# Casting the values in the DMA instead of on ScalarE, in an attention and expert kernel

## The chip, the cores and the metric

One Trainium2 chip; the kernel runs on one of its cores. The metric is the device time of one execution in microseconds. The engines are called as in the profile: PE (TensorE), ACT (ScalarE), DVE (VectorE), POOL (GpSimd) and SP (SyncE, which here only issues DMAs). SP, ACT and POOL can each issue DMAs; a DMA that changes the type of its data is issued from POOL in this kernel.

## The reference

Two layers follow each other. The first is attention with a relative-position bias; the second sends every token to one of eight experts by a hash of its id. Cut to what matters:

```python
# attention: B = 8 batches, H = 8 heads, S = 576 tokens, D = 64
scores = (1.0 / np.sqrt(D)) * np.matmul(q, k.transpose(0, 1, 3, 2))
scores = scores + bias_table[bucket(|i - j|)]        # one column of the table per head
attn = softmax(scores)
x = np.matmul(attn, v)                               # -> (B * S, H * D) = (4608, 512)

# experts: E = 8, w1 (E, 512, 1024), w2 (E, 1024, 512)
expert_idx = token_ids * 2654435761 % E
for e in range(E):
    mask = expert_idx == e
    out[mask] = np.maximum(x[mask] @ w1[e], 0.0) @ w2[e]
```

## The kernel before

The attention goes in 32 pairs of heads (8 batches x 4 pairs). The loop over `n` has one pass per pair and one more. In pass `n` the kernel computes the scores of pair `n` and the product of pair `n - 1` with its values; the inputs of later pairs are loaded, cast and transposed beside it. Keys are on the partitions, so the exponential on ACT writes the transposed attention that the value product takes as its stationary operand.

The values of a pair lie in a buffer `vt` (one of four): for each head four blocks of 128 keys, each block 64 value columns, a column of ones (its product is the softmax denominator) and zeros. The last 64 keys of a head are kept apart, in `vs`, for both heads of a pair together. Before the change v is loaded as float32 into `vf` by SP and cast into `vt` by ACT:

```python
VN = 98                       # width of a block of vt, and of the value product
vf = [at.tile([P, 2, NDUO, D], F32, name=f"vf{i}") for i in range(4)]
vt = [at.tile([P, 2 * (NDUO * VN + VO)], F16, name=f"vt{i}") for i in range(4)]

def load_v(n):
    b, m = pairs[n]
    for hh in range(2):
        nc.sync.dma_start(out=vf[n % 4][:, hh, :, :],
                          in_=v[b, 2 * m + hh, :NB4].rearrange("(t p) d -> p t d", p=P))

def cast_v(n):
    nc.scalar.activation(out=vt[n % 4][...][:, :, :, :D], in_=vf[n % 4][:, :, :, :],
                         func=AF.Copy, bias=0.0, scale=1.0)

def cast_vs(b):               # the tail of a batch, cast by POOL, two halves
    for hh in range(2):
        nc.gpsimd.tensor_copy(out=vs[b % 2][D * hh : D * hh + D, :, c0 : c0 + D],
                              in_=vsf[b % 2][D * hh : D * hh + D, :, :])
```

The scores of a group `g` go to PSUM (two buffers) and are exponentiated by ACT. `band` multiplies the part near the diagonal by the exponential of the bias, on DVE; `ebd` holds it, and `ebs` a compact copy for the last 64 keys:

```python
def scores(n, g):
    ...
    nc.scalar.activation(out=att[:, g, :, :], in_=ps[:, :, :QW], func=AF.Exp, ...)   # 128 x 1152

def band(n, g):
    ...                                       # g < 4: att *= ebd, one or two products
    nc.vector.tensor_tensor(out=a, in0=a, in1=ebs[:, :, m, :], op=ALU.mult)          # g == 4
```

At the end of a value product (`av_steps`) DVE takes reciprocals and scales. From pair 7 on POOL also clears a piece of the buffers for gathered rows there, and from pair 13 on it names slots: it scatters token numbers into a table in DRAM, one indirect DMA for each 128 tokens, 40 in all. A one-element copy of `rcp` paces them:

```python
if n >= 7 and (blank or unnamed):
    nc.gpsimd.tensor_copy(out=pace[:, :], in_=rcp[:1, 0, 0:1])
    if n >= 13:
        for _ in range(1 if ni == 2 else 2):
            if unnamed:
                name_slot(unnamed.pop(0))      # nc.gpsimd.indirect_dma_start(...)
    if blank:
        nc.gpsimd.memset(xf[...], 0)
```

The loop, cut to what the change touches:

```python
weights = [(w, e, w * y) for e in range(2) for w in (1, 2) for y in range(4)]   # 16 pieces
for n in range(NP + 1):                        # NP = 32
    av = iter(())
    if n > 0:
        av = av_steps(n - 1, finish if n == NP else None)
    if n == NP:
        first_inputs(0)                        # needs the rows gathered for expert 0
        advance(av, 99)
        ...
        break
    if 0 < n < NP - 4:
        load(n + 4, "qk" if n < 3 else "qkv")
    if b + 1 < B and m == 1: load_vs(b + 1)
    if b + 1 < B and m == 3: cast_vs(b + 1)
    if n == 28: ...                            # load the table of slots into xid
    if n >= 6 and pairs[n][1] != 0 and weights:
        w, e, y = weights.pop(0)
        (load_w1 if w == 1 else load_w2)(e, y, y + w)
    for g in range(NIT):                       # 5 groups
        scores(n, g)
        if n == NP - 2 and g == 1:
            gather(0, B - 1)                   # rows of expert 0 without the last batch
        if n == 0:
            if g == 1:   cast_k(1)
            elif g == 2: band(n, 0); band(n, 1)
            elif g == 3: transpose_q(1); transpose_k(1); band(n, 2)
            elif g == 4: band(n, 3); load(4, "qk")
        ...
        elif g == 0:
            transpose_k(n + 1); band(n - 1, NIT - 1); advance(av, 13)
        elif g == 1:
            cast_k(n + 2); cast_v(n + 1); advance(av, 14); band(n, 0)
        elif g == 2:
            cast_q(n + 3); advance(av, 9); band(n, 1)
        elif g == 3:
            transpose_q(n + 2); band(n, 2); advance(av, 99)
        else:
            band(n, 3)
```

After the loop the experts follow, one after the other: `hps` is the first product, `ops` the second, and the rows of the next expert are gathered and transposed beside them. The weights of experts 0 and 1 are loaded during attention, those of the others during the experts.

Of the kernel before, what the change touches and what calls it, by code (L numbers as in the profile page):

```python
# [31 lines left out]
def kernel(  # L32
# [145 lines left out]
    VO = HP - (VW - VN)  # L178
    NCH = S // D
# [3 lines left out]
    with tc.tile_pool(name="at", bufs=1) as at, tc.tile_pool(  # L183
# [3 lines left out]
        def aux(shape, dtype, name):  # L187
# [9 lines left out]
        qh, kh = {}, {}  # L197
        qf = [at.tile([PB, 2, NBLK, 2 * D], F32, name=f"qf{i}")
# [3 lines left out]
        vf = [at.tile([P, 2, NDUO, D], F32, name=f"vf{i}") for i in range(4)]  # L202
        vsf = [at.tile([P, NPAIR, D], F32, name=f"vsf{i}") for i in range(2)]
        vt = [at.tile([P, 2 * (NDUO * VN + VO)], F16, name=f"vt{i}")
              for i in range(4)]
# [7 lines left out]
        def load(n, what="qkv"):  # L213
            b, m = pairs[n]
            if what == "v":
                return load_v(n)
# [17 lines left out]
            if what == "qkv":  # L234
                load_v(n)

        def load_v(n):
            b, m = pairs[n]
            for hh in range(2):
                nc.sync.dma_start(  # L240
                    out=vf[n % 4][:, hh, :, :],
                    in_=v[b, 2 * m + hh, :NB4].rearrange(
                        "(t p) d -> p t d", p=P
                    ),
                )
# [25 lines left out]
        def cast_k(n):  # L271
# [4 lines left out]
            )  # L276

        def cast_v(n):
            nc.scalar.activation(  # L279
                out=vt[n % 4][:, :].rearrange("p (h y) -> p h y", h=2)[  # L280
                    :, :, : NDUO * VN
                ].rearrange("p h (t x) -> p h t x", t=NDUO)[:, :, :, :D],
                in_=vf[n % 4][:, :, :, :], func=AF.Copy, bias=0.0, scale=1.0,
            )
# [224 lines left out]
        def band(n, g):  # L509
# [22 lines left out]
            else:  # L532
# [3 lines left out]
                nc.vector.tensor_tensor(  # L536
                    out=a, in0=a, in1=ebs[:, :, m, :], op=ALU.mult
                )

        def av_steps(n, done=None):  # L540
            b, m = pairs[n]
            att, ats = atts[n]
            vb = vt[n % 4]
            for its in ((3, 4), (0, 1, 2)):
# [4 lines left out]
                for y, (ii, it, x) in enumerate(todo):  # L549
# [3 lines left out]
                    else:  # L553
# [7 lines left out]
                        v0 = (NDUO * VN + VO) * hh - VO * hh + VN * t  # L561
# [102 lines left out]
        keep_busy(bps[:, 2, :], 4)  # L664
# [8 lines left out]
        def v_init(i):  # L673
            nc.gpsimd.memset(vt[i][:, :].bitcast(I32), 0)
            nc.gpsimd.memset(
                vt[i][:, :].rearrange("p (h y) -> p h y", h=2)[
                    :, :, : NDUO * VN
                ].rearrange("p h (t x) -> p h t x", t=NDUO)[
                    :, :, :, D : D + 1
                ], 1.0,  # L680
# [18 lines left out]
        keep_busy(bps[:, 2, :], 4)  # L699
# [33 lines left out]
        for i in range(1, 4):  # L733
            v_init(i)
        nobody = at.tile([P, NSLOT // P, 2], I32, name="nobody")
        nc.gpsimd.memset(nobody[:, :, :], BIG)
        load_bias(nc.scalar, 0, 1, 0)
        load_bias(nc.sync, 0, 1, 1)
        load(0, "v")
        load_vs(0)  # L740
        load(2, "qk")
        for b2 in range(2):
            load_bias(nc.gpsimd, 1, NPAIR, b2)
        make_ebs(0, 1)
        cast_vs(0)
        make_ebs(1, NPAIR)
        transpose_q(0)
        keep_busy(bps[:, 2, :], 1)
        transpose_k(0)
        keep_busy(bps[:, 2, :], 1)  # L750
        cast_q(1)
        load(1, "v")
        load(3, "qk")
        load(2, "v")
        load(3, "v")
# [20 lines left out]
                   for e in range(2) for w in (1, 2) for y in range(4)]  # L776
        routing = route()
# [5 lines left out]
        for n in range(NP + 1):  # L783
# [9 lines left out]
            if 0 < n < NP - 4:  # L793
                load(n + 4, "qk" if n < 3 else "qkv")
            b, m = pairs[n]
            if n == 1:
                vs_init(1)
            if b + 1 < B and m == 1:
# [5 lines left out]
            if n == 28:  # L804
                assert not unnamed and not blank and not weights
# [4 lines left out]
            if n >= 6 and pairs[n][1] != 0 and weights:  # L810
                w, e, y = weights.pop(0)
                (load_w1 if w == 1 else load_w2)(e, y, y + w)
            for g in range(NIT):
# [9 lines left out]
                if n == 0:  # L823
                    if g == 1:
                        cast_k(1)
                    elif g == 2:
                        band(n, 0)
                        band(n, 1)
                    elif g == 3:
                        transpose_q(1)  # L830
                        transpose_k(1)
# [4 lines left out]
                elif n == 1:  # L836
                    if g == 0:
                        cast_v(0)
                        load_v(4)
# [13 lines left out]
                    else:  # L853
                        cast_v(1)
                        load_v(5)
# [8 lines left out]
                elif g == 1:  # L864
                    if n == 2:
                        transpose_q(3)
                        cast_v(2)
                        load_v(6)
# [239 lines left out]
```

## Time and profile before

| | us |
|---|---|
| median of three executions | 379.4 |
| the three | 378.36, 379.40, 380.87 |
| span of the profiled execution | 387.9 |
| in it: attention, to the first expert product | 231.4 |
| in it: experts | 156.5 |

The profiled execution is longer than the timed ones, so its stretches are compared with each other and with the profile of another kernel, and times with times. In a profile, a line such as `L492 ACT ACTIVATE att<-ps` is a group of instructions of line 492 on ACT that writes `att` from `ps`; a bracket at the end of a line is the idle time of that engine just before, and what ended it. The slots are named by the groups `t_id<-pay,ds`, the rows of an expert are gathered by `xg<-t_x,xid`, the attention's result is stored by `t_x<-x_all`.

| the values and what lies near them | engine | count | mean or median |
|---|---|---|---|
| exponential `att<-ps`, 128 x 1152 | ACT | 128 | 1129 ns |
| cast `vt<-vf`, 128 x 512 | ACT | 32 | 0.62 us |
| load `vf<-in_v_dram`, 128 KB | SP issues | 64 | - |
| slot `t_id<-pay,ds` | POOL | 40 | 1006 ns |
| weight piece `w1t`, 128 rows | POOL | 8 | 0.53 us |

### The profile page before, as it was taken

The numbers are of one execution on the slowest core, as the hardware profiler recorded it, in microseconds if no ns is written. First come the engines' busy times: TensorE is split into PE (matmuls) and PEld (weight loads), VectorE is DVE, ScalarE is ACT, GpSimd is POOL, SyncE is SP. The second block draws the span as 40 slices with busy tenths as digits, with TensorE's granted clock in tenths as the row PEclk, the third lists the DMA queues.
The fourth block names the chain that finished last, engine by engine and source line by source line (L and its number), as shares of the span: only waits on it lengthen the run. The fifth ranks groups of instructions, "written<-read, shape, count | busy, mean of one in ns | idle before, by whom it ended". The sixth has DMA issues, their size and how long they took to land.

```text
span 387.9 us, 8991 instructions
## 1 busy us (share of the span) xinstructions
PE 334.0 (86%) x3483; PEld 236.4 (61%) x3483; DVE 221.2 (57%) x617; ACT 241.1 (62%) x297; POOL 187.3 (48%) x300
## 2 busy tenths in 40 slices
PE   7578888898886889786887889989999999999991
PEld 2356767677675667574775676555656566665650
DVE  5679999999987999885797630303030202121121
ACT  2758888899986898784887716343535344544420
POOL 4622010131358758758625007587868585752322
PEclk9999999999999999996999899999999999999997
DMA  5999997888978998997642012939999999997212
GB/s 139 253 227 230 216 200 194 188 199 215 202 176 180 160 234 160 195 226 162 123 57 65 2 64 64 215 93 188 237 228 260 208 232 212 196 220 136 95 56 81
DMA packets 124854, 65.81 MB, mean 170 GB/s; under 512 B 85681, under 2 KB 117070, under 8 KB 124802
## 3 DMA queue, kind: packets, MB, share of 16 engines
q0 software_dynamic: 19584, 31.75, 40.4%
q1 hardware_dynamic: 104834, 33.18, 36.2%
q8 instruction: 29, 0.48, 0.5%
q10 hardware_dynamic: 384, 0.21, 0.2%
q14 instruction: 23, 0.19, 0.2%
HBM read 68.26 MB, written 15.30 MB: 215 GB/s over the span
## 4 chain that ended last, share of the span: by engine, by line
PE 60%; DVE 14%; ACT 11%; issue 9%; DMA 3%; SPq 0%; POOLq 0%; POOL 0%; DVEq 0%
PE hps L929 18%; PE ops L953 18%; PE px L563 9%; ACT att L492 8%; PE ps L484 6%; DVE att L525 4%; PE ps L488 3%; ACT vt L279 2%; DVE x_all L574 2%; PE xps L906 2%; PE pk L457 2%; PE xin L418 1%; DVE qh L264 1%; DMA t_x<-x_all 1%; DVE kh L273 1%
## 5 line engine op out<-in xcount | busy, mean ns | idle before, releaser
L492 ACT ACTIVATE att<-ps 128x1152 f16<-128x1152 f32 x128 | 141.0, 1129 | 41.4 <-PE ps L488 30.4
L484 PE MATMUL ps<-qt,kz 128*128 128x384 f16 x256 | 75.1, 333 | 26.6 <-ACT att L492 17.7
L960 DVE COPY ok<-ops 128x512 f32<-128x512 f32 x40 | 27.7, 692 | 122.2 <-PE ops L953 114.2
L563 PE MATMUL px<-vt,att 128*128 128x98 f16 x1280 | 83.3, 210 | 5.0 <-DVE x_all L574 2.4
L563 PEld LDWEIGHTS <-att 128*128 128x128 f16 x1280 | 71.0, 100 | 11.9 <-DVE x_all L574 3.5
L525 DVE TENSOR_TENSOR att<-att,ebd 128x384 f16<-128x384 f16 (+2 forms) x224 | 71.7, 357 | 5.8 <-ACT att L492 5.8
L953 PE MATMUL ops<-w2t,h 128*128 128x512 f16 x320 | 74.9, 379 | 0.0
L935 ACT ACTIVATE h<-hps 128x640 f16<-128x640 f32 x64 | 44.8, 704 | 39.5 <-PE hps L929 34.9
L929 PEld LDWEIGHTS <-w1t 128*128 128x128 f16 x512 | 50.1, 98 | 23.9 <-issue 3.5
L488 PE MATMUL ps<-qt,kz 128*128 128x192 f16 x256 | 63.9, 250 | 0.0
L929 PE MATMUL hps<-xpt,w1t 128*128 128x320 f16 x448 | 62.6, 299 | 1.4 <-issue 0.9
L961 POOL DMA_INDIRECT out_dram<-ok,xid x40 | 39.5, 988 | 47.9 <-DVE ok L960 41.9
L603 POOL DMA_INDIRECT t_id<-pay,ds x40 | 44.6, 1115 | 11.2 <-issue 10.1
L145 POOL DMA_INDIRECT xg<-t_x,xid x40 | 41.2, 1030 | 18.2 <-DMA t_x<-x_all 8.9
L953 PEld LDWEIGHTS <-h 128*128 128x128 f16 x320 | 30.1, 98 | 30.0 <-ACT h L935 0.2
L488 PEld LDWEIGHTS <-kz 128*128 128x128 f16 x256 | 25.3, 99 | 29.9 <-issue 29.5
L910 ACT ACTIVATE xpt<-xps 128x512 f16<-128x512 f16 x35 | 20.1, 596 | 36.4 <-PE xps L906 28.4
L563 PE MATMUL px<-vs,atts 128*128 128x132 f16 x160 | 35.8, 223 | 0.4 <-issue 0.4
L484 PEld LDWEIGHTS <-kz 128*128 128x128 f16 x256 | 25.3, 99 | 14.9 <-DVE kz L463 2.8
L574 DVE TENSOR_TENSOR x_all<-px,rcp 128x256 f16<-128x256 f32 x64 | 31.4, 491 | 2.2
L587 POOL COPY pace<-rcp 1x1 f32<-1x1 f32 x39 | 8.9, 229 | 46.1 <-DVE rcp L573 43.4
L257 POOL CAST vs<-vsf 64x256 f16<-64x256 f32 x16 | 7.4, 462 | 40.4 <-DMA vsf<-in_v_dram 26.5
(82 smaller groups left out, 346.9 us busy)
## 6 DMA issues: line engine op xcount, KB each, us to landing
qf<-in_q_dram SPq DMA_DIRECT2D x32, 288.0 KB
kf<-in_k_dram SPq DMA_DIRECT2D x32, 288.0 KB
vf<-in_v_dram SPq DMA_DIRECT2D x64, 128.0 KB
w1t<-in_moe_w_dram POOLq DMA_DIRECT2D x6, 1024.0 KB
w2t<-in_moe_w_dram POOLq DMA_DIRECT2D x6, 1024.0 KB
t_x<-x_all SPq DMA_DIRECT2D x7, 512.0 KB
w1t<-in_moe_w_dram POOLq DMA_DIRECT2D x8, 256.0 KB
w2t<-in_moe_w_dram POOLq DMA_DIRECT2D x8, 256.0 KB
```

Of the source, the lines that this page charges most:

```text
L145: nc.gpsimd.indirect_dma_start(out=xg[e % 3][:, sc, :], out_offset=None, in_=x_d.ap()[: S * nb, :], in_offset=bass.IndirectOffsetOnAxis(ap ...
L484: nc.tensor.matmul(out=ps[:, hh, :QW], lhsT=kt, rhs=qt[:, :QW], start=True, stop=True,)
L488: nc.tensor.matmul(out=ps[:, 2, RW * hh : RW * hh + RW], lhsT=kt, rhs=qt[:, QW:], start=True, stop=True,)
L492: nc.scalar.activation(out=att[:, g, :, :], in_=ps[:, :, :QW], func=AF.Exp, bias=0.0, scale=scale,)
L525: nc.vector.tensor_tensor(out=a, in0=a, in1=ebd[:, :, m, :, a0 + w0 : a1 + w0].transpose([0, 2, 1, 3]), op=ALU.mult,)
L563: nc.tensor.matmul(out=px[:, ii, o : o + w], lhsT=lhsT, rhs=rhs, start=(y == 0), stop=(y == len(todo) - 1), skip_group_check=True,)
L574: nc.vector.tensor_tensor(out=x_all[:, b, its[0] : its[0] + ni, P * m : P * m + P].rearrange("p t (h d) -> p t h d", h=2), in0=pv[:, :, :, ...
L603: i = nc.gpsimd.indirect_dma_start(out=id_d.ap()[:, :], out_offset=bass.IndirectOffsetOnAxis(ap=ds2[:, g : g + 1], axis=0), in_=pay[:, g, ...
L929: nc.tensor.matmul(out=hps[:, nr, :NR], lhsT=w1h[:, kt, ts(ft, P)], rhs=xt[e][:, kt, ts(nr, NR)], start=(kt == 0), stop=(kt == NPT - 1),)
L935: nc.scalar.activation(out=h1[:, ft, :].rearrange("p (r n) -> p r n", r=NRC), in_=hps[:, :, :NR], func=AF.Relu, bias=0.0, scale=1.0,)
L953: nc.tensor.matmul(out=ops[:, :], lhsT=h1[:, ft, ts(kc, P)], rhs=w2h[:, ft, :], start=(ft == 0), stop=(ft == NFT - 1),)
L961: so = nc.gpsimd.indirect_dma_start(out=out[:, :], out_offset=bass.IndirectOffsetOnAxis(ap=xid[:, NSC * e + kc, 1:2], axis=0), in_=ok[:, : ...
```

## The change

The values of the first 512 keys are no longer loaded as float32 and cast by ACT. A DMA from POOL reads them as float32 and writes float16 straight into `vt`. The blocks of `vt` are spread from 98 to 128 elements (256 bytes), the DMA writes 64 elements into each; the product still reads 98 columns of a block. `vf` and the cast are gone. The load of pair `n + 2` is issued in pass `n`, behind the value product of pair `n - 2`, which was the last to read that buffer.

```diff
+    VS = 2 * D
+    VY = (NDUO + 1) * VS
+        vt = [at.tile([P, 2, VY], F16, name=f"vt{i}") for i in range(4)]
-        vf = [at.tile([P, 2, NDUO, D], F32, name=f"vf{i}") for i in range(4)]
-        vt = [at.tile([P, 2 * (NDUO * VN + VO)], F16, name=f"vt{i}")
-              for i in range(4)]
         def load_v(n):
             b, m = pairs[n]
             for hh in range(2):
-                nc.sync.dma_start(
-                    out=vf[n % 4][:, hh, :, :],
+                nc.gpsimd.dma_start(
+                    out=vt[n % 4][:, hh, : NDUO * VS].rearrange(
+                        "p (t x) -> p t x", t=NDUO
+                    )[:, :, :D],
-        def cast_v(n):
-            nc.scalar.activation(...)
@@ av_steps
-                        v0 = (NDUO * VN + VO) * hh - VO * hh + VN * t
+                        v0 = VY * hh - VO * hh + VS * t
```

The weights of expert 0 (eight pieces) are loaded in every second pass from 7 to 21, those of expert 1 (eight pieces) in passes 27 to 31, instead of all sixteen in three passes of four from pass 6 on. This leaves POOL and the DMA engines free of weights in passes 22 to 26.

```diff
+        pieces = {7: 1, 9: 1, 11: 1, 13: 1, 15: 1, 17: 1, 19: 1, 21: 1,
+                  27: 1, 28: 1, 29: 2, 30: 2, 31: 2}
-            if n >= 6 and pairs[n][1] != 0 and weights:
+            if n + 2 < NP:
+                load_v(n + 2)
+            for _ in range(pieces.get(n, 0)):
                 w, e, y = weights.pop(0)
                 (load_w1 if w == 1 else load_w2)(e, y, y + w)
```

The start is put in another order. Pair 1 is cast and transposed two groups earlier, ahead of pair 0's bias products; both first bias loads are issued by SP, none by ACT; the compact copy `ebs` is made once in pass 3, and the first four pairs take their last group's bias from `ebd`, in two halves. The matmuls that keep PE busy before the first data write to a PSUM buffer of their own.

```diff
-        load_bias(nc.scalar, 0, 1, 0)
+        load_bias(nc.sync, 0, 1, 0)
         load_bias(nc.sync, 0, 1, 1)
-        make_ebs(0, 1)
+        load_v(1)
-        make_ebs(1, NPAIR)
+            if n == 3:
+                make_ebs(0, NPAIR)
@@ band, g == 4
+                if n < NPAIR:
+                    for hh in range(2):
+                        w0 = UB - HD * hh
+                        r = slice(D * hh, D * hh + D)
+                        nc.vector.tensor_tensor(out=a[r], in0=a[r],
+                            in1=ebd[r, :, m, hh, w0 : w0 + UB], op=ALU.mult)
+                else:
                     nc.vector.tensor_tensor(out=a, in0=a, in1=ebs[:, :, m, :], op=ALU.mult)
@@ pass 0
-                    if g == 1:
+                    if g == 0:
                         cast_k(1)
+                    elif g == 1:
+                        transpose_q(1)
+                        transpose_k(1)
                     elif g == 3:
-                        transpose_q(1)
-                        transpose_k(1)
                         band(n, 2)
```

(Cut: the first calls of `load_v`, the calls of `cast_v` in passes 1 and 2, the initialisation of the wider `vt`, and the lines that only change names.)

## The prediction

> **What bounds the kernel now.** I read the busy shares first, then the same busy times in four stretches, then the activations one by one to see how long a pass of the attention loop takes, and last the queue of POOL, because the change moves work there. The page, busy shares and the chain of waits:
>
> ```profile
> PE 334.0 (86%) x3483; PEld 236.4 (61%) x3483; DVE 221.2 (57%) x617; ACT 241.1 (62%) x297; POOL 187.3 (48%) x300
> ...
> PE 60%; DVE 14%; ACT 11%; issue 9%; DMA 3%; SPq 0%; POOLq 0%; POOL 0%; DVEq 0%
> ```
>
> No engine stands out over the whole span, because two programs follow each other: attention up to 231.4 us, experts after it. So I asked for the busy times by stretch (columns: length; then PE, PEld, DVE, ACT, POOL in us with the number of instructions; TensorE clock; DMA share; GB/s):
>
> ```profile
> 39.00:100.40 61.40, 52.63 (x765) 42.76 (x764) 59.66 (x184) 53.35 (x61) 8.76 (x31) 1.00 0.87 203
> 100.40:188.10 87.70, 70.50 (x988) 57.48 (x988) 74.03 (x221) 70.23 (x79) 60.28 (x98) 0.96 0.92 181
> 188.10:231.40 43.30, 35.52 (x466) 28.79 (x466) 30.99 (x94) 28.54 (x34) 11.18 (x13) 0.96 0.28 64
> 231.40:387.90 156.50, 147.24 (x972) 89.06 (x971) 27.67 (x40) 64.97 (x99) 91.49 (x117) 0.98 0.76 169
> ```
>
> From 39 to 100 us (passes 4 to 13) DVE is busy 59.66 of 61.40 us, 97%; ACT, which the change relieves, 87%. One undisturbed pass shows the same, DVE 5.65 of 5.80 us and ACT 5.36:
>
> ```profile
> 80.80:86.60 5.80, 5.12 (x77) 4.23 (x76) 5.66 (x18) 5.31 (x7) 3.12 (x9) 1.00 0.99 226
> 86.60:92.40 5.80, 5.19 (x79) 4.28 (x77) 5.65 (x19) 5.35 (x7) 0.62 (x4) 1.00 0.98 252
> ```
>
> Passes 14 to 26 (100.4 to 188.1 us) take 87.7/13 = 6.75 us each, although ACT, DVE and PE have no more to do. They have two disturbances of PE (its gaps near 122 and 176 us are put to "issue") and a POOL that names the slots of the tokens. POOL's instructions in order of time:
>
> ```profile
> 163.03 0.42 POOL L257 CAST vs<-vsf 64x256 f16<-64x256 f32 x1
> 168.40 0.40 POOL L257 CAST vs<-vsf 64x256 f16<-64x256 f32 x1 [4.95 <-DMA t_id<-pay,ds]
> ...
> 173.65 0.99 POOL L603 DMA_INDIRECT t_id<-pay,ds  x1 [0.30 <-issue]
> 174.63 0.18 POOL L587 COPY pace<-rcp 1x1 f32<-1x1 f32 x1
> 174.96 0.99 POOL L603 DMA_INDIRECT t_id<-pay,ds  x1 [0.16 <-issue]
> 175.95 0.18 POOL L587 COPY pace<-rcp 1x1 f32<-1x1 f32 x1
> 176.29 0.97 POOL L603 DMA_INDIRECT t_id<-pay,ds  x1 [0.16 <-issue]
> 177.57 0.97 POOL L603 DMA_INDIRECT t_id<-pay,ds  x1 [0.30 <-issue]
> 178.54 0.78 POOL L166 DMA_DIRECT2D w2t<-in_moe_w_dram  x1
> ...
> 205.47 1.07 POOL L145 DMA_INDIRECT xg<-t_x,xid  x1 [8.91 <-DMA t_x<-x_all]
> ...
> 267.74 0.84 POOL L158 DMA_DIRECT2D w1t<-in_moe_w_dram  x1
> ```
>
> The reader should see that POOL is issuing without a pause, 1.3 us a slot, and that every fourth pass its second cast of the values' tail waits 4 to 5 us until the slot DMAs have landed (3.59, 4.17 and 4.95 us). Between 103.4 us, its first act in pass 14, and 191.6, its first in pass 27, it waits only 2.2 us for DVE. The line at 205.47 is the gather of expert 0's rows, which still had time in hand; the last line is the issue of a 512-row load.
>
> **What the skill says.** "DMA: Bandwidth & Descriptors", section SWDGE vs HWDGE vs iDMA: a DMA that casts must be issued from GpSimd, whose software writes each descriptor, and only one such queue is allocated. The trace agrees as far as it goes: all casting weight loads are on POOL, 0.53 us for 128 rows, 0.84 us for 512. The same page, section Specifications, puts the line-rate minimum at 512 bytes; the values move as 256-byte reads and 128-byte writes. No row of this trace shows such a cast, so its cost to the DMA engines is open. "SBUF — State Buffer", section Who interferes with whom: a DVE copy or cast in a two-port mode and GpSimd's descriptor writing exclude each other. The slot DMAs, 975 ns at best, 1006 in the median and 1619 at worst, fit that but don't prove it.
>
> **Part 1, the cast leaves ACT.** 32 activations of 0.62 us, 19.8 us of ACT, go. In a pass ACT falls from 5.36 to 4.74 us; PE has about 5.1 and DVE 5.65 and neither loses anything. So the pass can shrink from 5.80 only to DVE's 5.65, of which I expect 0.1: 10 passes, 1.0 us. The periods above 5.8 us in passes 4 to 13 add up to 61.4 - 58.0 = 3.4 us. SP's queue waits 51.8 us in all for these casts, holding the q and k loads behind the v loads; with that gone I give half of the excess back, 1.7 us.
>
> **Part 2, the start.** ACT no longer issues the first two bias loads (8.50 to 9.82 us), so its first exponential comes about 0.4 us earlier. Pair 1's transposes no longer stand behind the bias products on DVE: the 1.71 us in which ACT sat idle before 16.33 us is filled. But SP now issues four bias loads one after the other, two more at 0.74 us, so bias and first products come some 1.4 us later, and pair 0's value products still follow them. Four tail products become two halves each, 4 x 0.26 us more. Sum: 1.5 us gained.
>
> Parts 1 and 2 up to pass 14: 1.0 + 1.7 + 1.5 = 4.2 us.
>
> **Part 3, POOL.** Two v loads a pass, 512 rows each; by the 0.84 us of the 512-row weight load I take 0.8 us. In passes 14 to 26 that is 26 x 0.8 = 20.8 us more. Nine weight pieces were issued there, four remain: 5 x 0.65 = 3.3 us less. POOL's own work from pass 14 to 27 was 88.2 - 2.2 = 86 us and becomes 103.5. Starting at 100.4 - 4.2 = 96.2, POOL reaches pass 27 at 199.7, against 191.6 before; undisturbed DVE-paced passes would be there at 96.2 + 13 x 5.7 = 170.3. The lead is three passes for v (loaded in pass n, used in n + 3) and two for the tail cast, 11 to 17 us: it is used up by about pass 21, and from there POOL sets the pace. Pass 29 needs the tail cast of pass 27: 199.7 + 0.85 + 1 to 4 of waiting, so it starts near 203, against 200.8 before.
>
> **Part 4, the end.** Passes 29 to 31 at 5.75 us put the start of the last stage at 220.3 (221.6 before). The first inputs of expert 0 need the gather. POOL must first do tail cast and waiting (3.5), the last slot (1.9), three pairs of v loads (4.8), six weight pieces (3.9) and the ramp (0.7): 199.7 + 14.8 = 214.5; five gathers of 1.3 end at 221, and the last lands some 4 us later behind 2 MB of queued weights, near 225. That is 3 to 4 us behind the 221.6 of before. The experts' 156.5 us do not change; expert 1's weights are needed 20 us into them. Sum of all parts with these sizes: +3.5, so 383.
>
> **Why I don't stay at 383.** Part 3 is a race with two soft sizes. If a v load costs 0.7 us (-2.6) and the three waits of 4 to 5 us shrink to 2.5 because five weight pieces are out of their way (-5), POOL is at pass 27 at 192 and the gather lands near 217.5: -4, 375. If instead DVE holds up the descriptor writing and a v load takes 1.0 us (+5.2), it is 388. The piece of the schedule that loads two weight pieces a pass from pass 29 looks fitted to a POOL that is free by then, so I weigh the light case a little more: 379.
>
> **Rivals.** (a) ACT was the bound and everything follows it: 0.6 us for each of 28 passes, 17 us, 362. For it: the chain of waits has ACT in every pass. Against it: DVE at 97%. (b) POOL paces passes 21 to 31 and delays the gather: 383 to 388. For it: the trace above; against it: the waits inside may be caused by the traffic that is moved. (c) The disturbances of 100 to 188 us come from weights and v loads crowding the DMA engines (share 0.92); with expert 1's 4 MB (as read) moved to where the share is 0.28, passes run at 5.8 and POOL just keeps up: 370 to 373. (d) 128-byte writes are so slow that v arrives late from the start: over 390; against it, three passes of lead.
>
> **Range and chances.** Middle 379, sizes of Part 3 alone give 375 to 388, rival (c) reaches 370: 369 to 388. Faster than 371.8 needs (a) or (c): 0.25. Slower than 387 needs the heavy (b) or (d): 0.17. Within: 0.58.
>
> **What would show it.** Right: DVE at 97% or more in passes 4 to 13 with a period of 5.65 to 5.75; POOL without a pause from pass 14 to 27 and v loads of 0.7 to 1.0 us; PE or ACT waiting for vt or vs around passes 22 to 29; the gather after 210 us and PE waiting for it at the first inputs. Wrong: DVE under 95% and passes under 5.6 us (Part 1 mis-sized); POOL waiting for DVE in passes 20 to 26 (Part 3); PE's gaps near 122 and 176 gone and the stretch under 80 us (rival c).

## The result and the profile after

| | median, us | lowest to highest | runs |
|---|---|---|---|
| before | 379.14 | 378.36 to 380.87 | 4 |
| after | 406.09 | 405.69 to 406.19 | 4 |

The changed kernel is slower: 1.0702 times the time before, 95% interval 1.0664 to 1.0740. The range of 369 to 388 us doesn't hold it. The two traces differ by less than the times do: the profiled execution of before spans 387.9 us, that of after 404.2, which is 16.3 us more. The traces can explain only these 16.3 us; the rest of the 27 us is taken up below with the first run.

The page of the kernel after, busy shares and the chain of work that ended last:

```profile
PE 339.1 (84%) x3483; PEld 239.8 (59%) x3483; DVE 222.4 (55%) x621; ACT 227.3 (56%) x265; POOL 238.0 (59%) x362
...
PE 40%; POOL 4%; issue 1%; DMA 1%; DVE 1%; ACT 0%; POOLq 0%; SPq 0%
```

ACT lost 13.8 us of work, POOL gained 50.7. The shares of the chain add up to 47% only: it is followed back no further than the end of the attention. But POOL, which had no part in the chain before, is in it. The same four stretches as before the change (the third now cuts off the end of the attention, because the experts start 15.8 us later, at 247.16 and not 231.40 us):

```profile
39.00:100.40 61.40, 52.69 (x764) 42.40 (x763) 59.86 (x185) 49.15 (x51) 23.40 (x52) 1.00 0.89 157
100.40:188.10 87.70, 70.76 (x1007) 58.24 (x1004) 74.25 (x225) 65.30 (x66) 68.20 (x106) 0.96 0.84 149
188.10:231.40 43.30, 29.52 (x376) 23.40 (x372) 29.33 (x92) 26.55 (x28) 27.33 (x37) 0.86 0.65 74
231.40:404.00 172.60, 157.65 (x1076) 97.03 (x1076) 31.27 (x48) 66.71 (x103) 95.47 (x122) 0.95 0.73 161
```

In the first two stretches about as many matmuls are done as before (764 and 1007, against 765 and 988). The third has 376 of them where it had 466: there the work is missing. The experts themselves take 404.2 - 247.2 = 157.0 us, against 156.5. Two undisturbed passes, the same columns:

```profile
78.90:84.70 5.80, 5.16 (x76) 4.25 (x76) 5.65 (x20) 4.96 (x6) 2.10 (x6) 1.00 1.04 186
84.70:90.50 5.80, 5.20 (x76) 4.25 (x76) 5.65 (x17) 4.84 (x6) 4.07 (x9) 1.00 0.81 191
```

ACT went from 5.3 to 4.9 us, DVE stayed at 5.65, and the pass stayed at 5.80. Now POOL near the end of the attention, in order of time (start, duration, instruction, and in brackets the idle time before it with what ended it):

```profile
202.13 0.97 POOL L602 DMA_INDIRECT t_id<-pay,ds  x1 [0.30 <-issue]
203.10 0.41 POOL L255 CAST vs<-vsf 64x256 f16<-64x256 f32 x1
204.45 0.57 POOL L255 CAST vs<-vsf 64x256 f16<-64x256 f32 x1 [0.94 <-issue]
204.96 1.59 POOL L236 DMA_DIRECT2D vt<-in_v_dram  x2
206.52 0.57 POOL L158 DMA_DIRECT2D w1t<-in_moe_w_dram  x1
207.14 0.18 POOL L586 COPY pace<-rcp 1x1 f32<-1x1 f32 x1
207.48 1.05 POOL L602 DMA_INDIRECT t_id<-pay,ds  x1 [0.16 <-POOL pace L586]
...
214.60 0.78 POOL L375 IOTA ramp<- 128x640 f16 x1
227.85 1.11 POOL L145 DMA_INDIRECT xg<-t_x,xid  x1 [12.48 <-DMA t_x<-x_all]
```

The last slot is named at 207.48 us. In the kernel before it was:

```profile
194.49 1.29 POOL L603 DMA_INDIRECT t_id<-pay,ds  x1 [0.16 <-POOL pace L587]
```

After the change POOL is through its queue at 215.4 and waits 12.48 us for `t_x<-x_all`, the store of batch 6's rows, before it may gather. The store is SP's, and SP issues in order. First after the change, then before:

```profile
212.56 0.38 SPq L804 DMA_DIRECT2D xid<-t_id  x1
213.04 11.16 SPq L617 DMA_DIRECT2D t_x<-x_all  x1
224.25 0.51 SPq L622 DMA_DIRECT2D t_x<-x_all  x1
```

```profile
196.99 0.37 SPq L806 DMA_DIRECT2D xid<-t_id  x1
201.44 0.36 SPq L618 DMA_DIRECT2D t_x<-x_all  x1
```

The load of the slot table `xid` stands ahead of the store and waits until the last slot has landed, 4.0 us after its issue ended. Only then comes the store, and its issue lasts 11.16 us; before, it was 0.36. In that time it stands beside the six weight pieces that POOL had issued from 206.5 us on. At the other end PE waits for the gather. Before, at the same place, it waited 0.62 us, and for ACT. After, then before:

```profile
230.71 0.29 PE L400 MATMUL xin<-ident,xg 128*128 128x128 f16 x1 [7.03 <-DMA xg<-t_x,xid]
...
235.91 0.29 PE L400 MATMUL xin<-ident,xg 128*128 128x128 f16 x1 [0.90 <-DMA xg<-t_x,xid]
```

```profile
221.60 0.44 PE L410 MATMUL xin<-ident,xg 128*128 128x128 f16 x5 [0.62 <-ACT att L492]
```

PE's and POOL's waits of that kind, up to the experts (total us, times, longest):

```profile
POOL pace L586 <- DVE rcp L572: 20.9, 13, 3.4
PE xin L400 <- DMA xg<-t_x,xid: 11.1, 5, 7.0
PE px L562 <- POOL vs L255: 6.8, 3, 3.0
PE px L562 <- DMA vt<-in_v_dram: 3.8, 4, 1.4
```

The first line is slack of POOL: of its 20.9 us, 3.8 lie after 100 us, so from there to the end of the slots POOL hardly waits for DVE; what it still waits for is its own slots, 7.8 us ahead of tail casts. In passes 21, 25 and 29 the products wait for the tail cast, and a few times for v itself.

Yet the passes came through almost in time. ACT's exponential of a pass's last 64 keys marks where each pass stands; these are passes 27 and 31 after the change, then before:

```profile
194.92 0.66 ACT L494 ACTIVATE atts<-ps 128x576 f16<-128x576 f32 x1
224.09 0.65 ACT L494 ACTIVATE atts<-ps 128x576 f16<-128x576 f32 x1
```

```profile
194.66 0.66 ACT L504 ACTIVATE atts<-ps 128x576 f16<-128x576 f32 x1
221.44 0.66 ACT L504 ACTIVATE atts<-ps 128x576 f16<-128x576 f32 x1
```

The changed kernel is 0.3 us behind in pass 27 and 2.7 us in pass 31. So 13.1 of the 15.8 us are lost behind the last pass, where PE has nothing to do until the rows are there.

### The profile page after: what moved, and what is told of

It reads as the page before. It is cut to its first block, busy times and chain, and to the rows that moved or that the text cites. A ratio compares the mean times of both kernels' runs of the same rounds, so it can differ in the third digit from the quotient of the medians.

```text
span 404.2 us, 8966 instructions
## 1 busy us (share of the span) xinstructions
PE 339.1 (84%) x3483; PEld 239.8 (59%) x3483; DVE 222.4 (55%) x621; ACT 227.3 (56%) x265; POOL 238.0 (59%) x362
## 5 line engine op out<-in xcount | busy, mean ns | idle before, releaser
L562 PE MATMUL px<-vt,att 128*128 128x98 f16 x1280 | 87.3, 214 | 14.2 <-DVE x_all L573 6.9
L562 PEld LDWEIGHTS <-att 128*128 128x128 f16 x1280 | 73.3, 102 | 31.8 <-issue 13.2
L474 PE MATMUL ps<-qt,kz 128*128 128x384 f16 x256 | 76.7, 339 | 14.7 <-ACT att L482 12.3
L236 POOL DMA_DIRECT2D vt<-in_v_dram x64 | 49.6, 785 | 27.0 <-PE px L562 25.1
L478 PE MATMUL ps<-qt,kz 128*128 128x192 f16 x256 | 64.8, 253 | 0.0
L562 PE MATMUL px<-vs,atts 128*128 128x132 f16 x160 | 36.7, 230 | 6.8 <-POOL vs L255 6.8
L478 PEld LDWEIGHTS <-kz 128*128 128x128 f16 x256 | 25.8, 101 | 19.2 <-issue 18.8
L474 PEld LDWEIGHTS <-kz 128*128 128x128 f16 x256 | 25.7, 100 | 12.7 <-DVE qt L440 1.5
L586 POOL COPY pace<-rcp 1x1 f32<-1x1 f32 x39 | 10.1, 259 | 21.2 <-DVE rcp L572 20.9
```

Of the source, the lines that this page charges most:

```text
L236: nc.gpsimd.dma_start(out=vt[n % 4][:, hh, : NDUO * VS].rearrange("p (t x) -> p t x", t=NDUO)[:, :, :D], in_=v[b, 2 * m + hh, :NB4].rearrange(
L474: nc.tensor.matmul(out=ps[:, hh, :QW], lhsT=kt, rhs=qt[:, :QW], start=True, stop=True,)
L478: nc.tensor.matmul(out=ps[:, 2, RW * hh : RW * hh + RW], lhsT=kt, rhs=qt[:, QW:], start=True, stop=True,)
L562: nc.tensor.matmul(out=px[:, ii, o : o + w], lhsT=lhsT, rhs=rhs, start=(y == 0), stop=(y == len(todo) - 1), skip_group_check=True,)
```

## The experiments

The theory after the traces: POOL's time is what the v loads cost. They make POOL over-full from pass 14, so the slots come late, and the slot table, the store and the gather with them. Rivals: the weights that now stand in front of the store; the order of the SP queue; the transfers of v (their landing, or the queue they share); the start.

The kernel before is not alike on all chips. It took 379 us where the result was measured, and 392 to 396 us on the five chips of these runs, while the changed kernel took 406 us on both that ran it. So every ratio below is to the kernel before on the chip of its own set. The ratios leave out executions over 1.5% above the fastest of the same kernel in their set, so that the kernel before counts with 9 of 33 executions beside `after_same`, and `b_best` with 3 of its 7; no trace of `a_vback`, `a_fix` and `b_best` is read, because such an execution was profiled.

### Both kernels again

`after_same` is the changed kernel, `before_same` the kernel before, without an edit.

> The changed kernel as it is, timed beside the others of this set so that each part can be set against it and against the kernel before on one chip. Expected: 404 to 407 us, 1.03 to 1.045 times the kernel before if that stands near 392 us again on this chip (the loss of 25 to 27 us was measured where before stood at 379 us).

> The kernel before as it is, for a profile on the chip of these runs, where it takes about 392 us and not 379 while the changed kernel takes 406 us on both. If the 13 us come from a pace (passes near 7.1 us instead of 5.8 somewhere before the experts, as the kernel with late weights showed in passes 15 to 22), its profile shows the longer passes and an engine that they wait for; if from a lower granted clock, the experts' stretch grows past 157 us. Ratio to before: 1.0 within 0.01.

Measured: 405.99 us, 1.0400 (1.0328 to 1.0473); and 395.1 us, 0.9936 (0.9883 to 0.9989). The last number is a caution: one and the same kernel came out 0.6% low, so ratios within 1% of each other are not told apart here. The trace of before on this chip spans 392.3 us, 4.4 more than the first. From pass 14 to pass 22 its passes take 7.2 us each and not 6.5, and its last slot ends at 200.45 us and not 195.78. So the extra of that trace lies where POOL names the slots (1155 ns each and not 1108). Why the kernel ran at 379 us unprofiled on the first chip no trace shows; it stays open, and with it some 11 of the 27 us.

### The weights behind the gather, the order of the SP queue, the tail casts

`a_hold`: expert 1's eight pieces are issued behind the gather.

```diff
-                  27: 1, 28: 1, 29: 2, 30: 2, 31: 2}
+                  31: 8}
```

> The changed kernel, with the eight weight pieces of expert 1 issued together in pass 31, behind the gather of expert 0's rows, instead of in passes 27 to 31. Theory (the weights stand in front of the store of the attention's result, on which the gather waits): the store's issue on SP, 11.16 us long in the changed kernel, takes about 0.5 us, the gather begins some 9 to 10 us earlier than 227.85 us, PE's wait for it shrinks from 11 to about 2 us, and the time is 396 us. Rival (the attention passes are what became slow): the store moves, the time stays over 403 us. Rival (the table of slots comes late, and it alone holds the gather): no change, 405 us.

`a_order`: the load of the slot table goes behind the store of batch 6.

```diff
-            if n == 28: nc.sync.dma_start(out=xid[...], in_=id_d...)
@@ pass NP - 3, g == 1
                     store(B - 2, 0, NIT)
+                    nc.sync.dma_start(out=xid[...], in_=id_d...)
```

> The changed kernel, with the load of the slot table on SP put behind the store of batch 6 instead of ahead of it; the weight pieces stay where they are. Theory (SP waits for the last slot until 212.56 us and the store, ready about 6 us earlier, waits behind it and then meets six weight pieces): the store is issued near 207 us and lands before 213, the gather begins near 216 us, and the time is 395 us. Rival (the store is slow because of the weights however early it is issued): the store's issue is still 8 us or longer and the time is 402 us. Rival (attention passes): over 403 us.

`a_vsact`: the casts of the values' tail go from POOL to ACT.

```diff
-                nc.gpsimd.tensor_copy(out=vs[...], in_=vsf[...])
+                nc.scalar.activation(out=vs[...], in_=vsf[...], func=AF.Copy)
```

> The changed kernel, with the cast of the values' tail on ACT instead of POOL. Theory (POOL is over-full from pass 14 on, and every fourth pass PE waits for this cast): PE's three waits for the tail cast (6.8 us in all) are gone, POOL no longer waits for slot DMAs (7.8 us) nor casts (8 x 0.4 us), so the last slot is named about 10 us earlier, near 198 us; the store is then ready before the slot table and meets fewer weight pieces. Passes 20 to 29 are shorter by 6 to 7 us, the gather 10 us or more earlier, the time is 392 us. Rival (the slow cast DMAs of v hold PE anyway): waits for vt take the place of waits for vs, and the time is 402 us or more.

`a_all`: the three edits together.

> The changed kernel with all three: weight pieces of expert 1 behind the gather, slot table behind the store, tail cast on ACT. Theory: the gather is no longer waited for, and passes run at DVE's 5.7 us from pass 4 on; from 406 take 11 us for the gather, 6.8 for the tail cast and 1 to 4 for waits on vt: 384 to 388 us, so most of the loss is explained and the kernel before is still about 6 us faster because of the start. Rival (casting v by DMA is itself slower than load and cast): over 393 us. If ACT's freed time counts for more than I think, under 378 us.

| kernel | us | ratio (95% interval) | last slot ends, us | gather starts | experts start |
|---|---|---|---|---|---|
| a_hold | 402.86 | 1.0272 (1.0180 to 1.0365) | 210.4 | 220.4 | 240.2 |
| a_order | 405.94 | 1.0367 (1.0284 to 1.0450) | 211.8 | 227.7 | 248.0 |
| a_vsact | 397.39 | 1.0153 (1.0074 to 1.0232) | 197.0 | 216.2 | 236.7 |
| a_all | 395.80 | 1.0087 (1.0056 to 1.0118) | 196.8 | 210.5 | 230.0 |

The theories had promised 396, 395, 392 and 384 to 388 us, and all four were too low. With the pieces held back the store's issue took 3.22 us instead of 11.16, and the experts began 7 us sooner. But they took 161.5 us instead of 157.0, because the first layer waited 4.1 us for a later store (its output takes the place of rows that are still being written out), probably because the eight pieces now come all at once. Of 7 us, 3 were left. The order of SP's queue gained no time. These are POOL's gather and SP's loads of `a_order`:

```profile
227.65 1.12 POOL L145 DMA_INDIRECT xg<-t_x,xid  x1 [8.97 <-DMA xid<-t_id]
```

```profile
205.03 0.38 SPq L617 DMA_DIRECT2D t_x<-x_all  x1
205.46 0.52 SPq L622 DMA_DIRECT2D t_x<-x_all  x1
215.33 0.36 SPq L815 DMA_DIRECT2D xid<-t_id  x1
```

The store left in time, and the wait changed its owner: the gather started at the same time as after the change, only now it waited for the slot table, whose load was issued at 215.33 us and had landed only then. (The last slot was also 3 us later than after the change, which the edit doesn't explain.) So the end is set by the last slot and by the weights in front of whatever must follow it. The tail casts on ACT pulled the last slot forward by 11.5 us, though this run lost 7 us at its start. ACT, in order of time:

```profile
14.91 0.42 ACT L255 ACTIVATE vs<-vsf 64x256 f16<-64x256 f32 x1 [9.77 <-DMA vsf<-in_v_dram]
```

Batch 0's tail arrives late, and the first exponentials stood behind its cast. That was an accident of the edit, and in the next set the cast of batch 0 stays on POOL.

### Where the weights go, and a mended version

`a_wbefore` puts the weights of the changed kernel back to before's passes, `b_late` puts the changed kernel's weights into the kernel before; `a_fix` is `a_all` with batch 0's tail cast on POOL.

```diff
-            for _ in range(pieces.get(n, 0)):      # a_wbefore: - to +; b_late: + to -
+            if n >= 6 and pairs[n][1] != 0 and weights:
```

> The changed kernel with only the weight loads put back to where before had them (one piece in nearly every pass from pass 6). Theory (the store of batch 6 stands behind the late slot table and then 11 us behind the weight pieces): the store's issue falls from 11.16 to under 1 us, the gather starts some 6 to 9 us sooner, the time falls by 5 to 9 us. Rival (GpSimd is over-full from pass 14 whatever is loaded late): the eight pieces now stand between the v loads and the slots at 0.7 us each, the last slot is named 4 to 6 us later than 207.5, and the time stays within 2 us of the changed kernel.

> The kernel before with only the weights' schedule of the changed kernel. Theory (late pieces hurt when a store on the sync queue and the gather must pass them): its store of batch 6 was issued at 201.4 and its gather ended at 211.8, 9.8 us before the first inputs needed it; with the pieces of passes 27 to 29 ahead of it the store's issue grows to 5 to 11 us, the gather ends at 219 to 224 and the time rises by 0 to 4 us. Rival (late pieces hurt by themselves, through traffic): 8 us or more. Rival (they free GpSimd and the queues in passes 14 to 27): the time falls by over 2 us.

> The three edits together (expert 1's last eight pieces behind the gather, the slot table's load behind the store of batch 6, the tail casts on ScalarE), but the tail cast of batch 0 left on GpSimd, because on ScalarE it held pass 0 back by 7 us. Theory (the three stand for the loss between pass 14 and the gather and the 7 us at the start were an accident of the edit): pass 0 at 14 us again, 386 to 391 us, 0.98 to 1.0 times before. Rival (passes 14 to 22 are paced by GpSimd at 6.6 us, and a start 7 us sooner only meets that pace sooner): 393 to 396 us.

`a_wbefore`: 406.81 us, 1.0389 (1.0302 to 1.0476), nothing gained, as the rival had it. The last slot ended at 216.1 us, 7.3 later than in `after_same`, since the pieces now stood between the slots; and from the last slot to the first expert it took 29.7 us instead of 37.7. POOL must issue the pieces somewhere, and what they cost in one place they give back in the other. `b_late`: 393.52 us, 1.0076 (1.0028 to 1.0124). The late pieces by themselves cost the kernel before 0.8%, and 1.2% at most. They do lengthen the store (SP of `b_late`):

```profile
207.39 4.25 SPq L618 DMA_DIRECT2D t_x<-x_all  x1
211.70 1.93 SPq L623 DMA_DIRECT2D t_x<-x_all  x1
```

but the gather still came in time, because the last slot was there at 200.2 us: PE's first inputs waited for ACT and not for it. `a_fix`: 389.62 us, 0.9920 (0.9878 to 0.9962), within what theory gave.

### The v loads undone, and POOL's time alone

`a_vback` undoes only the v loads: v comes by SP as float32 and is cast by ACT into the new blocks; the late weights and the new start stay.

```diff
-                nc.gpsimd.dma_start(out=vt[n % 4][...], in_=v[...])
+                nc.sync.dma_start(out=vf[n % 4][:, hh, :, :], in_=v[...])
+            cast_v(n): nc.scalar.activation(out=vt[n % 4][...], in_=vf[n % 4][...], func=AF.Copy)
```

> The changed kernel with one part undone: v comes as float32 on the sync queue again and is cast by ScalarE, into the new 256-byte blocks; late weights and the new order of the start stay. Theory (the v loads on GpSimd are what costs most): the last slot is named before 199 us, no pass waits for v or the tail cast for more than 1 us, and the time comes to that of before with late weights (393.5 us) plus the 1 to 3 us of the start: 393 to 397 us. Rival (late weights, the blocks' layout or the start cost it): it stays above 402 us.

Measured: 396.43 us, 1.0008 (0.9960 to 1.0057). With the v loads gone from POOL the whole loss is gone; the new start and the late weights together cost nothing that shows.

What of the v loads costs: their time on POOL, or their transfers? `a_pad` and `a_pad3` add to `a_vback` two or three idle POOL instructions per pass, which move no data through a DMA. `a_vdum` adds the same casting v loads, into a buffer that nobody reads, so no matmul waits for them.

```diff
+            if n + 2 < NP:
+                for _ in range(2):                 # a_pad3: 3
+                    nc.gpsimd.iota(dum[:, :], pattern=[[1, 640]], base=0, channel_multiplier=0)
@@ a_vdum instead
+                for hh in range(2):
+                    nc.gpsimd.dma_start(out=dum[:, :, hh, :], in_=v[...])
```

> The kernel with v back on the sync queue and ScalarE (396.43 us), and in the place of each pass's two v loads two idle instructions of GpSimd that fill a buffer nobody reads (128x640 f16, 0.7 to 0.9 us each in the traces, as long as a v load's 0.785). No transfer moves, only GpSimd's time is taken. Theory (the cost of the v loads is their 1.6 us of GpSimd's time in each pass): the passes from 14 on and the last slot go back to the changed kernel's, the store's issue grows to some 10 us, and the time comes to 403 to 408 us. Rival (it is the transfers: the queue that v shares with the slots and weights, or their landing late): 396 to 399 us.

> The kernel with v on the sync queue and ScalarE (1.0008 of before), with three idle GpSimd instructions of 0.70 us in each pass, 2.1 us where the two v loads took 1.6 and where two of them (1.4 us) gave 1.023. Theory (GpSimd's time in a pass sets the time): beyond the changed kernel's 1.04, 1.04 to 1.06, some 408 to 416 us. Rival (half of the loss is from transfers, GpSimd's time alone gives about 5 us for 1.4): 1.03 to 1.04, 404 to 408 us.

> The kernel with v on the sync queue and ScalarE (1.0008 of before), with each pass's two v loads by GpSimd as well, cast into a buffer that nobody reads and nobody waits for. Both GpSimd's time and the transfers are there, but no matmul waits for their landing. Theory (the cost is GpSimd's time and what follows from it, and the transfers add the rest through the weights' queue): 1.03 to 1.05, 404 to 411 us, with the store's issue at 10 us or more. Rival (the last third of the loss is matmuls that wait for v to land): 1.02 to 1.025 like the kernel with idle instructions, 400 to 402 us.

POOL's groups between 100 and 188 us, first of `a_pad`, then `a_pad3`, `a_vdum` (busy us, mean ns):

```profile
L822 POOL IOTA dum<- 128x640 f16 x22 | 15.5, 703 | 1.0
```

```profile
L822 POOL IOTA dum<- 128x640 f16 x31 | 22.8, 735 | 1.7
```

```profile
L823 POOL DMA_DIRECT2D dum<-in_v_dram x20 | 16.3, 821 | 4.2 <-issue 2.7 <-DVE qh L270 1.1 <-DMA dum<-in_v_dram 0.2
```

So the doses are 2 x 0.70 = 1.4, 3 x 0.735 = 2.2 and 2 x 0.82 = 1.6 us a pass. With `b_late`, which has the late weights alone, and the changed kernel:

| kernel | POOL, us a pass | ratio (95% interval) | us | last slot ends | store's issue | experts start | from slot to experts |
|---|---|---|---|---|---|---|---|
| b_late | 0 | 1.0076 (1.0028 to 1.0124) | 393.52 | 200.2 | 4.25 | 237.0 | 36.8 |
| a_pad | 1.4, idle | 1.0231 (1.0177 to 1.0285) | 401.08 | 207.0 | 6.66 | 243.8 | 36.8 |
| after_same | 1.6, v | 1.0400 (1.0328 to 1.0473) | 405.99 | 208.9 | 10.19 | 246.6 | 37.7 |
| a_vdum | 1.6, v unread | 1.0434 (1.0351 to 1.0517) | 410.18 | 214.6 | 4.45 | 252.6 | 38.0 |
| a_pad3 | 2.2, idle | 1.0540 (1.0457 to 1.0624) | 413.69 | 219.4 | 4.50 | 255.3 | 36.0 |

In the last four of these kernels PE waits for the gather (6.8 to 9.4 us in all), and there the last column is the reading: with weights in front, the experts start 36 to 38 us after the last slot, whatever the store's issue took; in `a_hold` and `a_wbefore`, where PE waits for the gather too but no weights are in front, 29.8 and 29.7. So the late weights cost some 7 us at this place, in one form or another, and about as much is paid for them elsewhere. (`b_late` is no such case: the end of its passes sets its 36.8 us, as in the kernel before, which has 35.6 without weights in front.) Once the gather is waited for, what moves the time is when the last slot is named, and that is later with more of POOL's time per pass, moved data or not.

How much of the loss is POOL's time can only be estimated. `a_pad`, which moves no data on POOL for its 1.4 us, has 2.3%, and neither range expected of it holds its 401.08 us. On a straight line between the two doses of idle time, the 1.6 us of the v loads would give 1.023 + (0.2/0.8) x 0.031 = 1.031. The changed kernel had 1.040, its interval begins at 1.033; with the bias load moved (`a_bias`, below) it had 1.036 on the chip of `a_pad`, and `a_vdum` had 1.043. By plain times the line gives 404.2 us, 1.8 short of 405.99. So some three quarters to nine tenths of the loss come from POOL's time alone; the rest, half a percent to one percent, may be the transfers, or a bend between the two doses. A bend is likely: pass 31 stands at 221.72 us in `a_pad`, so that its loss lies behind the passes, but at 236.22 in `a_pad3`. Nor are the idle instructions quite without a side effect: DVE's cast of k took 629 ns in the mean in `a_pad` and 700 in `a_pad3` from 39 to 188 us, against 599 in `b_late` and 578 after the change.

That matmuls wait for v to land is at most a small part: in the changed kernel they wait 3.8 us for it in all, and pass 27 was in time. `a_vdum`, where nobody waits for it, was no faster, but it loads v twice, by SP for ACT's cast and by POOL, and with the dose of the changed kernel its last slot ends 6 us later (214.6 us) and its pass 31 stands at 233.43; so it doesn't settle this. The store's issue stayed at 4.45 us there, against the 10 expected; that part of the expectation failed.

How POOL's time gets into the passes at the larger loads is seen in the waits of `a_pad3` and `a_vdum` from 100 to 240 us:

```profile
DVE rcp L580 <- POOL pace L594: 21.1, 9, 6.5
...
PE px L570 <- POOL vs L263: 8.2, 3, 5.5
```

```profile
DVE rcp L580 <- POOL pace L594: 11.3, 6, 4.0
...
PE px L570 <- POOL vs L263: 9.1, 3, 5.6
```

POOL's one-element copy `pace` reads the reciprocals, which keeps it from running ahead of DVE. The buffers of the reciprocals are four, two a pass, so when POOL falls two passes behind the same copy holds DVE back, and through it PE and ACT.

### The start

`a_bias`: the changed kernel with the first bias load issued by ACT again.

```diff
-        load_bias(nc.sync, 0, 1, 0)
+        load_bias(nc.scalar, 0, 1, 0)
```

> The changed kernel with only the first half of the first bias load issued by ScalarE again. Theory (the late start comes from that load standing on the sync queue, and is then lost or kept whole up to the gather): pass 3 starts 1 to 3 us sooner than 40.8 us, but the gather still waits on the store behind the last slot, so the time stays within 2 us of 406. Rival (the start is carried to the end): 403 to 404 us. Rival (the order of the queue is not the cause): pass 3 within 0.5 us of the changed kernel's.

A wait of the first 41 us is 3.3 us long in the changed kernel and 1.4 us in `a_bias`:

```profile
DVE att L515 <- DMA ebd<-t_f: 3.3, 1, 3.3
```

```profile
DVE att L515 <- DMA ebd<-t_f: 1.4, 1, 1.4
```

Pass 3 has its first tail exponential at 38.23 us, against 40.79 after the change and 38.39 before, so most or all of the late start comes from this load on SP's queue. The time is 405.49 us, 1.0359 (1.0300 to 1.0419): nothing of it arrives at the end. What is gained ahead of a queue that is over-full is swallowed by it.

### Versions that might beat both

`b_vsact`: the kernel before with the tail casts from batch 1 on ACT. `a_fixb`: `a_fix` with the first bias by ACT. `a_best2`: `a_fixb` with the thirty fills of the gather's buffers done three at a time in passes 7 to 12. `b_best`: `b_vsact` with the same.

```diff
-                    if blank:
+                    for _ in range(3 if n < 13 else 1):
+                        if not blank:
+                            break
                         i, j = blank.pop(0)
```

> The kernel before with one edit: from batch 1 on the tail casts of v go to ScalarE, so that GpSimd no longer waits for its slot writes to drain in front of them (8 us of such waits in passes 15 to 22 before). Theory (GpSimd paces those passes even before): faster by 2 to 6 us, 386 to 390 us. Rival (GpSimd has slack there and ScalarE only gets 0.6 us more per cast): within 2 us of before, and no pass shorter.

> The kernel with the three edits and the tail cast of batch 0 on GpSimd (389.62 us), with the first half of the first bias load issued by ScalarE again, as before. Theory (the start of the changed kernel is late because the first bias load stands on the sync queue behind other loads): pass 3 starts about 2 us sooner and the time is 387 to 389 us, 0.98 to 0.99 of before. Rival (passes 14 to 22 are paced by GpSimd and swallow it): 389 to 391 us.

> The kernel of 390.83 us (v by casting loads, last eight weight pieces behind the gather, the slot table's load behind the store, tail casts from batch 1 on ScalarE, first bias by ScalarE), with the thirty fills of the gather buffers done three at a time in passes 7 to 12, where GpSimd is busy 40 per cent, and not one at a time through pass 21. Theory (passes 14 to 22 go at GpSimd's pace of 6.6 us, of which the fills are 0.5): those passes go at 6.1 us and the time falls by 3 to 5 us, 386 to 388 us. Rival (the fills disturb VectorE, which is full in passes 7 to 12): within 1 us or slower.

> The kernel before with the tail casts from batch 1 on ScalarE (392.76 us, 0.991 of before) and the thirty fills done in passes 7 to 12. Theory (GpSimd paces passes 15 to 22 of the kernel before too, near 7 us in these runs): those passes shorten by 0.4 to 0.5 us each, 386 to 390 us, 0.975 to 0.985 of before. Rival (they are bound by ScalarE, which casts v there): 392 to 393 us.

| kernel | us | lowest to highest | ratio (95% interval) |
|---|---|---|---|
| b_vsact | 392.76 | 388.48 to 396.03 | 0.9911 (0.9882 to 0.9941) |
| a_fixb | 390.83 | 390.04 to 394.14 | 0.9875 (0.9796 to 0.9954) |
| a_best2 | 389.21 | 387.11 to 391.43 | 0.9921 (0.9893 to 0.9949) |
| b_best | 392.09 | 385.78 to 395.94 | 0.9842 (0.9784 to 0.9899) |

All four lie 0.8 to 1.6% below the kernel before, not far from the 0.6% by which it missed itself; the theories of the first three had promised 1 to 3 us more. `a_best2` has the narrowest spread; in its trace the last slot ends at 191.1 us and the experts start at 227.0, earlier than in any other trace that is read, though they then take 158.6 us. In `a_best2` passes 14 to 22 still go at 6.6 us each, not the 6.1 expected, so half a microsecond less on POOL did not shorten them; why is not shown. `a_fixb` was expected to start pass 3 some 2 us sooner, and had it at 42.3 us, later than the changed kernel's 40.8: the gain of `a_bias` did not repeat there. A version of the change that keeps its parts and doesn't lose exists; one that beats the kernel before by over 2% was not found.

## Why the prediction was wrong

- Part 1, right in its bound and wrong in its sum: DVE is at 59.86 of 61.40 us, 97%, and passes take 5.80 us with or without ACT's cast. The ten passes from pass 3's mark take 61.57 us against 61.87: 0.3 gained, not 2.7. SP's wait behind the casts gave nothing back that shows.
- Part 2, wrong in sign: pass 3 comes 2.4 us later, not 1.5 sooner. The sum was wrong by itself: its four terms, 0.4 + 1.71 - 1.4 - 4 x 0.26, make -0.3 and not 1.5. Beyond that `a_bias` shows that the bias load on SP was the larger term; without it pass 3 comes 2.6 us sooner than in the changed kernel. It didn't matter at the end.
- Part 3, right about POOL: v loads took 0.785 us in the mean (0.8 taken), POOL waits for DVE only 3.8 us from 100 us on, the products wait for the tail cast from pass 21 on, where the lead was said to end. (The passes lost little by it, 0.3 us up to pass 27.) POOL reaches the tail cast of pass 27 at 203.1 us (199.7): the loop was some 6 us later at pass 13 than Parts 1 and 2 had promised, and POOL had 3 us less to do than I reckoned. Of the Trainium skill's page "SBUF — State Buffer", section Who interferes with whom, no more is seen than before: slots took 1117 ns in the mean from 100 to 188 us, and 1108 before the change.
- Part 4, the step that failed: the gather was reckoned by POOL's own queue and 4 us of weights, so it would be issued at 214.5 and land near 225. POOL was indeed through its queue at 215.4. But the gather was issued at 227.85 and PE had its last rows at 235.9. From the end of the last slot to the gather I had 9.4 us, and it was 19.3: 4.0 until the slot has landed and SP may load the table, 0.5 for that load, 11.7 to issue the store behind it among the weights, 3.1 until it has landed. The prediction knew of SP's queue only its waits for v; the order, slot table ahead of store, was already there before the change. `a_hold` shows what the weights do in it: without them the store's issue took 3.22 us.
- "Why I don't stay at 383" made it worse by 4 us. Of its two light sizes one came true: the three waits for the slots took 7.8 us in all, 2.6 each, as the light case had it. The other didn't: a v load took 0.785 us, not 0.7. The light case failed because the gather doesn't follow POOL's own queue. `a_pad` to `a_pad3` show how steep the dependence is: 0.8 us a pass more on POOL is 3% of the time.
- Rival (b) was the right one in its second half, the delayed gather, and its 383 to 388 too low for the same reason as Part 4; that POOL paces passes 21 to 31 shows in waits for the tail cast, but costs little. Rivals (a), (c), (d) fell: the undisturbed pass stayed at 5.80 us; the stretch from 100.4 to 188.1 us has the same matmuls in it with the weights moved away; v was never late before pass 14.

With these two terms put right, 3.4 us later at the last slot and 9.9 more from there to the gather, the +3.5 us of the sum becomes +16.8; the traces differ by 16.3. That the two are so close is in part luck, since three smaller errors cancel: the rows were there 8.1 us after the first gather was issued and not 10.5; from there to the first expert product it took 11.3 us and not the 9.8 of before (PE's granted clock was 0.50 from 226 to 239 us, and its first ten `xin<-hot,x_all` products took 2.88 us, the later tens 1.52); and the experts took 0.5 us longer. The prediction set its sum on 379.4 us, and the trace of before spans 387.9: what separates these two was not found.

## What to carry to other kernels

Moving work to an engine with 48% busy time is safe only where that 48% lies elsewhere: take the engine's busy time in the stretch where it must do it, and follow its last product through every in-order queue to the instruction that waits for it. An idle instruction of the same length on the receiving engine gives a first measure of such a move before it is written (here 2.3% for 1.4 us a pass, where the move cost 4.0% for 1.6). When a wait is removed and the next one ends at the same time, as with `a_order`, the cause is upstream of both.

## What was not expected of the hardware

- The issue of one 512 KB store on SP took 0.36 us in the kernel before, 3.38 (`a_vsact`) to 11.16 us where casting weight loads had been issued by POOL just ahead of it, and 3.22 and 3.66 in `a_hold` and `a_wbefore`, where only v loads had. SP issues nothing else in that time.
- The same kernel takes 379 us on one chip and 392 to 396 on five others, and the changed one 406 on both it ran on. Of the two, the kernel with slack on POOL is the one that varies.
